# Sliding-window attention and a mixture of experts on one core: the sums of weights move on GpSimd, the half tile's code moves ahead of the full tile's, one tile's turn of x moves

## The chip, the core and the metric

The kernel runs on one NeuronCore of a Trainium2 chip. The metric is the device time of one execution in microseconds (us). Before the change three executions took 769.08, 773.89 and 774.53 us, median 773.89.

The engines of the core run their own instruction streams and meet at semaphores: PE (TensorE, matrix products; its weight loads are shown as PEld), DVE (VectorE), ACT (ScalarE), POOL (GpSimd, which here also issues the gathers and scatters) and SP (SyncE, which issues plain DMAs).

## What is computed

```python
# attention: q, k, v of (8, 8, 576, 64), causal window of 64
scores = where(0 <= i - j < 64, q @ k.T / sqrt(D), -1e9)
attn   = softmax(scores) @ v               # -> x of (4608, 512)
# mixture of experts, one expert per token, E = 8, F = 1024
logits = x @ w_gate;  expert_idx = argmax(logits, axis=1)
gate_w = softmax(logits)[n, expert_idx]
for e in range(E):                         # rows of the tokens of expert e
    h = maximum(x_sorted[lo:hi] @ w1[e], 0)
    y_sorted[lo:hi] = h @ w2[e]
return gate_w[:, None] * y                 # in the tokens' order
```

With the inputs of this case the experts get 669, 400, 748, 505, 592, 390, 566 and 738 tokens.

## The kernel before

**Two parts.** The first (up to about 215 us of the profiled span, with a mixed stretch to 247 us) is the attention. It writes x, already weighted with the gate, to `x_dram`. The second handles tokens expert by expert in *tiles* of 256 slots. Each product of a tile is made with seven smaller products instead of eight (a Strassen scheme), which needs sums and differences of the quarters of the weights and of x.

**A full tile** has these steps, in `body` (L481):

- `finish` (L422): three DVE additions (helper line L380) that complete the output `ys` of the tile *before*.
- `scatter` (L287): POOL copies the token numbers (L288) and issues two indirect DMAs (L291) that write `ys` to `out`.
- `hidden` (L332): PE makes seven products (L340), each 16 matmul records of 128x128. DVE and ACT evict between them (L350, L357, L361, L366, L371 on DVE). Into this stretch DVE also takes twelve of the 16 *transposes* (L311, `turned_blocks`) of the next tile's x, in the slots given by `some(blocks, n)`.
- `output` (L389): DVE forms four sums of the hidden values (`left_sums`, L139), makes the remaining transposes, and PE makes seven products (L384). ACT copies the turned x (L323), DVE forms the sums of the next tile's x (`sums_x`, L329).
- `gather` (L268): after the first product of `output`, POOL copies token numbers (L269) and issues two indirect DMAs (L271), which fetch the x of the tile after the next into the buffer that the transposes have just read.

**A half tile** (`half_tile`, L433) holds up to 160 tokens and is made with plain products: L441 (64 matmul records), L459, L469, L459, with its evictions at L449 and L451, 16 transposes, a gather after them, and L323 and L329 at its end.

**Which tiles run.** Each expert has `tiles` and `fulls`, read into registers at run time. Here they are (3,2), (2,1), (3,3), (2,2), (3,2), (2,1), (3,2), (3,3). Numbering experts from 0 and tiles from t0, the order is: expert 0 two full tiles, which are written out without a test ("first" and "second tile"), then a half one; expert 1 full, half; expert 2 three full; expert 3 two full; expert 4 two full, half; expert 5 full, half; expert 6 two full, half; expert 7 three full. The first tile of experts 1 to 7 is unconditional, all later ones stand inside nested tests made by `more` (L1069).

**Sums of weights.** On POOL, `sums_w1(e)` and `sums_w2(e)` are four operations of 128x1024 each (POOL rows of L139). `hidden` reads the first, `output` the second, whose last sum `t[3]` is used by the second of its products. `sums_w2(e)` stands ahead of the first `body` of expert e, so behind the last gather of expert e-1. `sums_w1(e+1)` stands behind the first tile of expert e. Weights are loaded by SP (L156, L159) at the head of an expert, into buffers of which there are two.

**Order.** Everything is in a schedule written by hand: each engine runs its instructions in the order of the program.

## Time and profile before

| | |
|---|---|
| executions | 769.08, 773.89, 774.53 us |
| the profiled execution | 780.25 us, of it span 778.5 us |
| mean granted TensorE clock over the span | 0.971 |
| a full tile in its undisturbed form, PE start to PE start | 381.53 to 406.12 us: 24.6 us |
| a half tile | 673.40 to 691.39 us: 18.0 us |
| last PE matmul ends, last scatter issued | 766.3 us, 775.2 us |

The profile is of one execution. A row of a group gives busy time and mean ns of one, then the idle time of the engine just ahead of the group and what ended most of it. A row of the timeline gives the start in us from the span's start, the length in us, the engine, the line, the operation with its output and input tiles, how many were merged, and in brackets the idle time ahead of it with what ended it; "issue" means that the profile shows nothing that the engine waited for.

### The profile page before, as it was taken

Reading aid. Unit: us, or ns where it says so; the run is one execution under the profiler, and the core shown is the slowest. Engines: PE = TensorE matmul, PEld = TensorE weight load, DVE = VectorE, ACT = ScalarE, POOL = GpSimd, SP = SyncE. Lnnn points to the kernel's source line nnn. Section 1 sums busy time; section 2 is a strip of 40 time slices with the busy share of each in tenths; the row PEclk is TensorE's granted clock in tenths of the full one; section 3 lists DMA queues with packets and bytes.
Section 4 is the critical chain, followed back from the end, with each engine's and each line's share of the span. In section 5 each row is a group of like instructions: output and inputs, shape, how many; then the busy total and the mean of one; then the engine's idle time right before and its main releaser. Section 6 shows DMA issues by size and latency. Waiting matters only on the chain. (4 is left out here: it accounts for less than half of the span.)

```text
span 778.5 us, 18249 instructions
## 1 busy us (share of the span) xinstructions
PE 707.8 (91%) x6962; PEld 635.1 (82%) x6962; DVE 528.6 (68%) x1654; ACT 267.0 (34%) x676; POOL 356.9 (46%) x366
## 2 busy tenths in 40 slices
PE   5999999999799789998999699899888989999993
PEld 3888888887698678888999599799777879889993
DVE  2677998989667636859667267368496686676862
ACT  4888888887451111102122012022011111112210
POOL 5215476694842426276631534644266527263112
PEclk9999999999999889999999899899999999999997
DMA  8998889883533515144120710711341611111011
GB/s 161 223 203 180 176 204 241 189 237 111 165 108 131 183 59 208 56 149 166 28 69 22 265 28 29 267 35 48 138 154 32 224 62 55 57 30 51 24 42 56
DMA packets 137638, 94.71 MB, mean 122 GB/s; under 512 B 117072, under 2 KB 117072, under 8 KB 137490
## 3 DMA queue, kind: packets, MB, share of 16 engines
q1 hardware_dynamic: 127858, 62.16, 29.4%
q0 software_dynamic: 9056, 28.58, 11.2%
q10 hardware_dynamic: 576, 2.10, 0.8%
q8 instruction: 80, 1.31, 0.8%
q14 instruction: 68, 0.56, 0.2%
HBM read 73.94 MB, written 20.45 MB: 121 GB/s over the span
## 5 line engine op out<-in xcount | busy, mean ns | idle before, releaser
L271 POOL DMA_INDIRECT qk_m<-x_dram,at_g x42 | 45.0, 1070 | 235.6 <-DVE v_m L311 227.4
L311 DVE STREAM_TRANSPOSE v_m<-qk_m 32x256 f32<-32x256 f32 x320 | 139.3, 435 | 12.7 <-DMA qk_m<-x_dram,at_g 7.7
L340 PE MATMUL bank<-qk_m,s 128*128 128x128 f32 x1024 | 129.7, 285 | 19.9 <-DVE qk_m L350 11.7
L340 PEld LDWEIGHTS bank<-qk_m,s 128*128 128x128 f32 x1024 | 124.8, 201 | 21.2 <-issue 14.5
L340 PE MATMUL bank<-qk_m,w 128*128 128x128 f32 x768 | 97.9, 283 | 9.7 <-issue 6.0
L340 PEld LDWEIGHTS bank<-qk_m,w 128*128 128x128 f32 x768 | 94.5, 199 | 11.4 <-issue 10.9
L650 ACT ACTIVATE pr<-pr,mx 128x128 f32<-128x128 f32 x288 | 89.7, 390 | 33.6 <-DVE mx L640 33.3
L640 DVE CUSTOM_DVE_ANT_0 pr<-bank,mask 128x128 f32<-128x128 f32 x288 | 64.4, 285 | 28.5 <-PE bank L627 27.2
L380 DVE TENSOR_TENSOR v_m<-bank,v_m 128x256 f32<-128x256 f32 x95 | 38.2, 420 | 47.2 <-PE bank L384 30.7
L291 POOL DMA_INDIRECT out_dram<-v_m,at_s x42 | 42.4, 1009 | 33.9 <-DVE v_m L380 20.7
L441 PE MATMUL bank<-qk_m,w 128*128 128x160 f32 x320 | 47.9, 312 | 9.7 <-issue 9.7
L139 POOL TENSOR_TENSOR s<-w 128x1024 f32<-128x1024 f32 x22 | 52.7, 2397 | 7.9 <-DMA qk_m<-x_dram,at_g 5.0
L441 PEld LDWEIGHTS bank<-qk_m,w 128*128 128x128 f32 x320 | 46.4, 199 | 12.0 <-issue 12.0
L329 DVE TENSOR_TENSOR qk_m<-v_m,qk_m 128x256 f32<-128x256 f32 x60 | 45.1, 778 | 13.6 <-ACT qk_m L323 13.0
L568 POOL COPY v_m<-v_m 64x520 f32<-64x520 f32 x32 | 19.8, 618 | 67.8 <-DMA v_m<-in_v_dram 65.2
L673 PEld LDWEIGHTS bank<-v_m,pT 128*64 128x64 f32 x1152 | 40.7, 139 | 12.1 <-DVE xs L687 6.0
L673 PE MATMUL bank<-v_m,pT 128*64 128x65 f32 x1152 | 47.4, 230 | 3.1 <-DVE xs L687 3.1
L384 PE MATMUL bank<-qkT_m,v_m 128*128 128x256 f32 x216 | 48.3, 379 | 0.0
L627 PE MATMUL bank<-qkT_m 64*64 64x128 f32 x1152 | 45.8, 290 | 0.1
L384 PEld LDWEIGHTS bank<-qkT_m,v_m 128*128 128x128 f32 x216 | 41.0, 190 | 5.5
L347 ACT COPY qk_m<-bank 128x512 f32<-128x512 f32 x16 | 9.4, 586 | 104.2 <-PE bank L340 86.1
L594 PE MATMUL bank<-ident,qk_m 128*128 128x128 f32 x256 | 36.7, 287 | 7.7 <-POOL mask L516 4.9
(174 smaller groups left out, 1289.0 us busy)
## 6 DMA issues: line engine op xcount, KB each, us to landing
w<-in_moe_w_dram SPq DMA_DIRECT2D x11, 2048.0 KB, 8.5
qk_m<-in_q_dram SPq DMA_DIRECT2D x72, 128.0 KB, 3.6
qk_m<-in_k_dram SPq DMA_DIRECT2D x72, 128.0 KB, 3.6
v_m<-in_v_dram SPq DMA_DIRECT2D x64, 128.0 KB, 3.7
qk_m<-in_moe_w_dram SPq DMA_DIRECT2D x3, 2048.0 KB, 14.3
x_dram<-xs POOLq DMA_DIRECT2D x6, 512.0 KB, 4.9
x_dram<-xs POOLq DMA_DIRECT2D x3, 768.0 KB, 6.1
w<-in_moe_w_dram ACTq DMA_DIRECT2D x4, 512.0 KB, 4.9
```

Source lines behind the costliest of these rows:

```text
L139: op()
L271: G.indirect_dma_start(out=xg[c], out_offset=None, in_=x_dram[:, :], in_offset=bass.IndirectOffsetOnAxis(ap=at_g[:, c : c + 1], axis=0),)
L291: put = G.indirect_dma_start(out=out[:, :], out_offset=bass.IndirectOffsetOnAxis(ap=at_s[:, c : c + 1], axis=0), in_=ys[c], in_offset=None ...
L311: V.transpose(out=xn[b * QD : (b + 1) * QD, :, :, a * QD : (a + 1) * QD].rearrange("p c g i -> p (c g) i"), in_=rows[a * QD : (a + 1) * QD ...
L329: V.tensor_tensor(out=xs[:, n], in0=a, in1=b, op=ALU.subtract)
L340: nc.tensor.matmul(acc[:, f, :], lhsT=a[:, g, f * P : (f + 1) * P], rhs=b[:, g, :], start=(first and f == 0 and g == 0), stop=(g == HG - 1 ...
L384: nc.tensor.matmul(acc, lhsT=a[:, f, :], rhs=b[:, f, :], start=(start and f == 0), stop=(stop and f == HF - 1), skip_group_check=True,)
L441: nc.tensor.matmul(acc[:, i], lhsT=w1[:, g, f * P : (f + 1) * P], rhs=xq[:, g].rearrange("p c s -> p (c s)")[:, 0:HALF], start=(i + g == 0 ...
L627: nc.tensor.matmul(out_, lhsT=qT[rows, t, a * WINDOW : (a + 1) * WINDOW], rhs=rhs, start=True, stop=True, skip_group_check=True,)
L640: V.tensor_tensor_reduce(out=prs[h][:, m, :], in0=scs[h][:, m, :], in1=mask[:, m0 + m, :], scale=-scale, scalar=-2 * MASKED, op0=ALU.add, ...
L650: nc.scalar.activation(out=y, in_=y, func=AF.Exp, scale=-1.0, bias=mx[:, h, m : m + 1])
L673: nc.tensor.matmul(px[a * D : (a + 1) * D, h, m, :], lhsT=pTs[h][:, m, a * D : (a + 1) * D], rhs=vt[:, h, :], start=True, stop=True, skip_ ...
```

## The change

Three edits:

1. `body` takes a function `between`, called after the scatter and ahead of the transposes and the gather. `sums_w2(e)` is handed to the first tile of expert e, `sums_w1(e + 1)` to the next one of the expert (for expert 0, to its half tile), whichever form it has; where there is no such tile a new Else arm calls it. So each set of four POOL operations leaves its old place and stands between L291 and L269 of one tile. Their number doesn't change.
2. The inner test gets `preferred_fallthrough_block=False`. In the built program the half tile's block then stands directly behind the test and the full tile's block behind it, with everything nested in it. Before, the full block with all nested tiles stood first, and each level's half block after all of that.
3. In the second tile of expert 0, `hidden` no longer gets `blocks`: all 16 transposes of that tile are made in `output`, after its `left_sums`.

```diff
-    def body(e, last, after, full):
+    def body(e, last, after, full, between=None):
 
         finish()
         scatter(perm_i[:, last])
+        if between is not None:
+            between()
         blocks = turned_blocks()
...
-        tile1 = chain(hidden(0, blocks), output(0, blocks))
+        tile1 = chain(hidden(0), output(0, blocks))
...
-            if e:
-                sums_w2(e)
-
...
-            def more(n):
-
-                with tc.If(tiles > n):
-                    with tc.If(fulls > n) as full:
-                        body(e, *place(n), True)
+            def more(n, between=None):
+
+                with tc.If(tiles > n) as some_left:
+                    with tc.If(fulls > n, preferred_fallthrough_block=False) as full:
+                        body(e, *place(n), True, between)
                         if n + 1 < KT:
                             more(n + 1)
                         else:
...
                     with full.Else():
-                        body(e, *place(n), False)
+                        body(e, *place(n), False, between)
+                if between is not None:
+                    with some_left.Else():
+                        between()
 
             if e:
-                body(e, *place(0), True)
-            if e + 1 < E:
-                sums_w1(e + 1)
-            more(1 if e else NE)
+                body(e, *place(0), True, partial(sums_w2, e))
+            more(1 if e else NE, partial(sums_w1, e + 1) if e + 1 < E else None)
```

## The prediction

> **What bounds the kernel now.** I read the page first, then the timeline of PE alone over the expert part, then all engines around each gap, then instruction fetches in small windows.

> ```profile
> PE 707.8 (91%) x6962; PEld 635.1 (82%) x6962; DVE 528.6 (68%) x1654; ACT 267.0 (34%) x676; POOL 356.9 (46%) x366
> L340 PE MATMUL bank<-qk_m,s 128*128 128x128 f32 x1024 | 129.7, 285 | 19.9 <-DVE qk_m L350 11.7
> L329 DVE TENSOR_TENSOR qk_m<-v_m,qk_m 128x256 f32<-128x256 f32 x60 | 45.1, 778 | 13.6 <-ACT qk_m L323 13.0
> ```

> PE bounds the expert part: an undisturbed full tile takes 24.6 us from PE start to PE start, with PE never idle. So what can be won is PE's gaps. Summed over the tiles from 246 us on they are about 60 us against 24.6 (full) and 18.0 (half), and come in three kinds.

> First kind, ends of half tiles. L329 has a mean of 778 ns, yet takes 0.42 us in undisturbed tiles:

> ```profile
> 616.14 6.71 DVE L329 TENSOR_TENSOR qk_m<-v_m,qk_m 128x256 f32<-128x256 f32 x3 [0.23 <-ACT qk_m L323]
> 617.66 2.41 POOL L139 TENSOR_TENSOR qkT_m<-qk_m,qkT_m 128x1024 f32<-128x1024 f32 x1
> 622.77 2.56 DVE L329 TENSOR_TENSOR qk_m<-qk_m,v_m 128x256 f32<-128x256 f32 x1
> 627.38 5.15 PE L340 MATMUL bank<-qk_m,s 128*128 128x128 f32 x32 [3.07 <-DVE qk_m L350]
> ```

> The four L329 (both inputs in SBUF) take turns with POOL's four L139, which start after the last gather; finish and L350 queue behind them on DVE, and PE waits for L350.

> Second kind, the second tile:

> ```profile
> 257.33 2.68 DVE L311 STREAM_TRANSPOSE v_m<-qk_m 32x256 f32<-32x256 f32 x6 [6.22 <-DMA qk_m<-x_dram,at_g]
> 262.43 3.79 PE L340 MATMUL bank<-qk_m,s 128*128 128x128 f32 x16 [4.97 <-DVE qk_m L361]
> ```

> DVE stands at the transposes until the gather has landed, and L357 and L361 behind them free PE's banks late.

> Third kind, borders between blocks:

> ```profile
> 283.34 6.90 PE L441 MATMUL bank<-qk_m,w 128*128 128x160 f32 x29 [3.08 <-issue]
> ...
> 436.19 3.38 PE L340 MATMUL bank<-qk_m,w 128*128 128x128 f32 x16 [5.31 <-issue]
> 441.93 2.27 PE L340 MATMUL bank<-qk_m,s 128*128 128x128 f32 x12 [1.91 <-issue]
> 494.38 3.75 PE L340 MATMUL bank<-qk_m,w 128*128 128x128 f32 x16 [3.71 <-DVE v_m L380]
> 770.00 1.27 DVE L380 TENSOR_TENSOR v_m<-bank,v_m 128x256 f32<-128x256 f32 x3 [6.29 <-DMA out_dram<-v_m,at_s]
> ```

> These follow jumps. In windows of about a microsecond the queue "q8 instruction" moves one 16 KB packet at such a place, so I read them as code loading: one at 428.0 to 429.5, two more at 431.0 to 432.5, then PE starts at 436.19. Reading the packets' times against PE's next start, a load from a jump costs 2.7 (half tile at 335.0), 3.3 (548.2), 3.0 (597.5) and 2.9 us (673.4); PE's sequencer is some 2 us ahead of its array, so 0.99, 1.45, 1.16 and 0.62 us show, mean 1.05.

> [...]

> ```profile
> 335.00:344.00 9.00, 9.00 (x66) 8.97 (x67) 6.52 (x17) 0.57 (x1) 7.87 (x7) 1.00 0.11 42
> 436.00:440.00 4.00, 3.81 (x20) 3.78 (x21) 0.00 (x0) 0.35 (x1) 4.00 (x3) 0.62 1.03 400
> ```

> The third number from the end is the granted clock: 1.00 against 0.62.

> **Edit 1, the sums.** Nothing is added; 14 sets of four L139 (4 x 2.35 = 9.4 us) move. Room in a full tile:

> ```profile
> 407.56 1.00 POOL L291 DMA_INDIRECT out_dram<-v_m,at_s  x1 [0.70 <-issue]
> 408.54 0.22 POOL L269 COPY at_g<-perm_i 128x2 int32 x1
> 425.44 1.24 POOL L271 DMA_INDIRECT qk_m<-x_dram,at_g  x1 [16.68 <-DVE v_m L311]
> ```

> The tile's PE start is 406.12: sums could run from +2.5 to +12 us, and the gather behind them on POOL waits for DVE until +19.3 anyway. In a half tile the gather is free at +13.2, so about 1 us is left; later than that, it has some 4 us until the next tile's first transposes. Moved past scatters, the sums also release them: in the tiles after sums_w1 (472.55) the scatter came 5 us late, which nobody waited for; gain zero. In +2.5 to +12 all DVE work is L311 (one input) or evictions with a PSUM input. While POOL ran its old sums at 463 to 472 us those kept their 0.44 and 0.69 us, so I cost the overlap at zero.

> Gain: PE's waits for L350 are 11.7 us (five, the page's row); 1.4 more at 620.50 for L329; the slow matmuls after two of them (5.28 and 5.15 for 3.74) 2.9. Together **16.0**.
> [...] Trace: 2.57 for 0.42 us beside sums of 2.35 to 2.54, so each waits a whole one. [...]
> The new wait: t[3], the *last* of sums_w2, is used at +14.2 (420.36). Before, it was long done. Where a tile follows a half one, finish will come late after a jump (below): end of L329 at about -0.5, 3.2 us of loading, 1.3 of finish, scatter until +5, sums until +14.7. Cost 0.5 us in each of five first tiles, **-2.5**; bounds 0 and -10 (2 us each).

> **Edit 3.** From 246.49 to 279.43 the second tile took 32.9 us, 8.3 too many. Without transposes DVE follows PE through hidden; left_sums end at about +16.8, 16 transposes (0.45 each, 7.2) at +24.0, ACT's copies (1.1) at +25.2, 0.6 to 0.8 after PE could go on. The half tile's transposes wait for a gather issued after them (landing at about 277, median 4.1 us after issue), so its L449 is late by some 0.7. Gain **6.8**; bounds 3 (the gather later still) and 8.

> **Edit 2, the blocks.** A half tile is 160 matmul records and 160 weight loads, a full one 168 and 168. [...]

> Won at entries of half tiles: 0.45 + 3.08 and slow matmuls (11.9 for 8.93) at 280, and 0.99, 1.45 + 0.53, 1.16 + 1.44, 0.62: 6.4 + 6.2 = 12.6. Lost at their exits: four at 0.9 (I take the entry's 1.05 less a longer lead), less the 0.71 that expert 4's exit cost already. [...] Net 12.6 - 3.6 + 0.7 - 4.5 = **5.2**.

> [...]

> Ends of experts without a half tile. Before, two jumps in a row: to the arm of the failed test, and on over the half blocks behind it. After, the second has nothing to pass. Expert 2 to 3: 5.31 + 1.91 + 3.1 of slow matmuls; I leave 0.8 + 1.9 (a block's end is 44 instructions on, and the weights' load is running) + 1.3: gain 6.3. Expert 3 to 4: 3.71 + 3.0 slow, leave 0.8: gain 5.9. Tail: DVE's finish at 770.00 after 6.29 us, about two loads; with one it starts at 766.9: gain 3.1. **15.3**, bounds 5 and 18. [...] For a block end met badly I take **-1**.

> Sum: 16.0 - 2.5 + 6.8 + 5.2 - 3.2 + 15.3 - 1 = 36.6, say 37. The profiled execution, 780.25 us, becomes 743; it lies 0.8% above the median shown, so 773.89 - 37 = **737 us**.

> **Rivals.**
> - *The jumps only move the stalls* (0.14). Entries against exits and double against single jumps cancel, and all seven full jumps show: 16.0 + 6.8 - 7.4 - 2.5 = 13, **761 us**. For it: equal loads, each about 3 us. Against: two-jump chains are in the trace and become one.
> - *Loading is hidden better* (0.08): exits and full jumps free, no late sums: 37 + 8 + 3 + 2.5, **724 us**. For it: expert 4's and 6's old exits showed 0.71 and 0.
> - *The sums come too late in first tiles* (0.05): seven tiles have PE waiting for t[3]. If each L139 took twice its time beside DVE, a set would end at +21.4, 7.2 us late, seven times 50: **787 us**, slower than before. The gain is gone from 5.3 us per tile, when an L139 takes over 4.2 us. Against: 2.34 to 2.54 us beside transposes.
> - *The order of blocks isn't what it says* (0.01): the built program has the half block first.

> **How the numbers follow.** Forecast 0.72 (its own range 726 to 749). The range 724 to 757 leaves out most of the first and third rival. One per cent, about 8 us, is what this measurement can tell from none. Forecast, hidden loading and nearly all of the first rival are faster: 0.93; within 1%: 0.03; slower: 0.04.

> **What would show it.** Right: L329 at 0.42 us throughout and no PE wait for L350 at half tiles; PE's gaps of 5.31 and 3.71 down to about 1; the second tile near 25 us; DVE's last finish within 1 us of PE's end; a double stall at the start of expert 7. Wrong: PE waiting for POOL's L139 by more than 1 us a tile, or gaps over 2 us at jumps into full tiles.

## The result, and the profile after

The changed kernel takes 744.11 us (median of 4 runs, 741.95 to 745.06) against 774.21 us for the kernel before in the same comparison: ratio 0.9615, 95% interval 0.956 to 0.9669. On another chip it gave 741.56 against 773.32 us, ratio 0.9577 (0.9532 to 0.9622). So it saves 30 to 32 us; the prediction said 37 and 737 us. All medians here are of executions in the faster of the chip's two states; of `turn_only` below, two of ten were in the slower one and are left out.

The two profiled executions differ by more, 778.5 to 740.2 us of span, because that of before lay some 6 us above its median and that of after 2 us below. Every place read below comes from single executions, which differ from one another by a few us, and the comparison of totals from the medians.

The page of the changed kernel, first the engines, then two groups (busy us, mean ns | idle us ahead of the group and what ended most of it):

```profile
PE 695.1 (94%) x6962; PEld 625.4 (84%) x6962; DVE 496.7 (67%) x1654; ACT 267.3 (36%) x676; POOL 355.7 (48%) x366
L340 PE MATMUL bank<-qk_m,s 128*128 128x128 f32 x1024 | 124.7, 278 | 0.6 <-issue 0.6
L340 PE MATMUL bank<-qk_m,w 128*128 128x128 f32 x768 | 96.0, 279 | 11.8 <-issue 8.1
```

and the last of these groups as it was before:

```profile
L340 PE MATMUL bank<-qk_m,w 128*128 128x128 f32 x768 | 97.9, 283 | 9.7 <-issue 6.0
```

VectorE's busy time fell by 31.9 us with the same 1654 instructions, and 19.9 us of idle time ahead of the products with `s` fell to 0.6. That ahead of the products with `w`, the first of which opens a full tile, rose from 9.7 to 11.8: stops at jumps moved there. VectorE wasn't the bound; what counted is which of its instructions were late. L329 alone, its shortest, median and longest duration in ns:

```profile
L329 DVE TENSOR_TENSOR qk_m<-v_m,qk_m x60: 415/424/427, 270.6 to 723.5; 128x256 f32<-128x256 f32 x60
```

None of the 60 is over 0.43 us, where the mean before was 0.78.

What is left of TensorE's waits from the second tile on, in the timeline of PE (start, length, idle time ahead of it in brackets with what ended it):

```profile
272.56 2.73 PE L384 MATMUL bank<-qk_m,v_m 128*128 128x256 f32 x8 [3.40 <-DVE v_m L380]
...
295.39 2.02 PE L340 MATMUL bank<-qk_m,w 128*128 128x128 f32 x16 [1.47 <-DMA qk_m<-x_dram,at_g]
...
339.05 2.02 PE L340 MATMUL bank<-qk_m,w 128*128 128x128 f32 x16 [1.15 <-issue]
...
414.51 2.02 PE L340 MATMUL bank<-qk_m,w 128*128 128x128 f32 x16 [1.22 <-DVEq L1070]
...
417.55 1.50 PE L340 MATMUL bank<-qk_m,s 128*128 128x128 f32 x12 [0.57 <-issue]
...
465.54 2.02 PE L340 MATMUL bank<-qk_m,w 128*128 128x128 f32 x16 [0.88 <-DVEq L1070]
...
480.53 1.99 PE L384 MATMUL bank<-qkT_m,qk_m 128*128 128x256 f32 x8 [0.52 <-POOL qkT_m L139]
...
535.73 3.05 PE L340 MATMUL bank<-qk_m,w 128*128 128x128 f32 x16 [1.92 <-issue]
538.57 2.59 PE L340 MATMUL bank<-qk_m,s 128*128 128x128 f32 x16
...
580.75 2.02 PE L340 MATMUL bank<-qk_m,w 128*128 128x128 f32 x16 [0.88 <-issue]
...
648.38 1.02 PE L340 MATMUL bank<-qk_m,w 128*128 128x128 f32 x7 [0.53 <-issue]
651.64 1.49 PE L340 MATMUL bank<-qk_m,w 128*128 128x128 f32 x9 [2.24 <-issue]
652.92 3.40 PE L340 MATMUL bank<-qk_m,s 128*128 128x128 f32 x16
...
703.30 2.05 PE L340 MATMUL bank<-qk_m,w 128*128 128x128 f32 x16 [1.36 <-issue]
```

The reader is to see three things. The wait of 3.40 us in the second tile is new. The 5.31 and 3.71 us at the borders from expert 2 to 3 and 3 to 4 became 1.22 and 0.88. And a full tile behind a half one now pays at its start, as at 535.73, or twice, as at 648.38 and 651.64 after seven matmul records. (The gather named at 295.39 is not what this tile waits for: in `bank3_order` below it starts at 293.85 after 0.75 us, while VectorE gets that gather's rows only at 301.80.)

The end of the run didn't move. VectorE still waits ahead of its last finish:

```profile
731.78 1.27 DVE L380 TENSOR_TENSOR v_m<-bank,v_m 128x256 f32<-128x256 f32 x3 [6.15 <-DMA out_dram<-v_m,at_s]
```

### The profile page after: what moved, and what is told of

Read it like the earlier page. It is cut to its first block, busy times and chain, and to the rows that moved or that the text cites. A ratio compares the mean times of both kernels' runs of the same rounds, so it can differ in the third digit from the quotient of the medians.

```text
span 740.2 us, 18250 instructions
## 1 busy us (share of the span) xinstructions
PE 695.1 (94%) x6962; PEld 625.4 (84%) x6962; DVE 496.7 (67%) x1654; ACT 267.3 (36%) x676; POOL 355.7 (48%) x366
## 3 DMA queue, kind: packets, MB, share of 16 engines
q0 software_dynamic: 9056, 28.58, 11.8%
## 5 line engine op out<-in xcount | busy, mean ns | idle before, releaser
L311 DVE STREAM_TRANSPOSE v_m<-qk_m 32x256 f32<-32x256 f32 x320 | 139.3, 435 | 5.2 <-DMA qk_m<-x_dram,at_g 0.3
L340 PE MATMUL bank<-qk_m,s 128*128 128x128 f32 x1024 | 124.7, 278 | 0.6 <-issue 0.6
L271 POOL DMA_INDIRECT qk_m<-x_dram,at_g x42 | 45.0, 1072 | 165.0 <-DVE v_m L311 155.9
L340 PEld LDWEIGHTS bank<-qk_m,s 128*128 128x128 f32 x1024 | 120.6, 195 | 0.6 <-issue 0.6
L340 PE MATMUL bank<-qk_m,w 128*128 128x128 f32 x768 | 96.0, 279 | 11.8 <-issue 8.1
L340 PEld LDWEIGHTS bank<-qk_m,w 128*128 128x128 f32 x768 | 91.0, 194 | 15.9 <-issue 15.7
L380 DVE TENSOR_TENSOR v_m<-bank,v_m 128x256 f32<-128x256 f32 x95 | 38.2, 420 | 55.3 <-PE bank L384 24.9
L291 POOL DMA_INDIRECT out_dram<-v_m,at_s x42 | 42.5, 1013 | 61.5 <-DVE v_m L380 47.2
L139 POOL TENSOR_TENSOR s<-w 128x1024 f32<-128x1024 f32 x22 | 52.2, 2373 | 0.0
L384 PE MATMUL bank<-qkT_m,v_m 128*128 128x256 f32 x216 | 48.3, 379 | 0.0
L384 PEld LDWEIGHTS bank<-qkT_m,v_m 128*128 128x128 f32 x216 | 41.0, 190 | 5.5
L441 PEld LDWEIGHTS bank<-qk_m,w 128*128 128x128 f32 x320 | 45.1, 194 | 0.4
L441 PE MATMUL bank<-qk_m,w 128*128 128x160 f32 x320 | 45.3, 303 | 0.0
L660 PE MATMUL bank<-ident,pr 128*128 128x128 f32 x288 | 43.8, 290 | 0.0
```

The costliest lines, as they stand in the source:

```text
L139: op()
L271: G.indirect_dma_start(out=xg[c], out_offset=None, in_=x_dram[:, :], in_offset=bass.IndirectOffsetOnAxis(ap=at_g[:, c : c + 1], axis=0),)
L291: put = G.indirect_dma_start(out=out[:, :], out_offset=bass.IndirectOffsetOnAxis(ap=at_s[:, c : c + 1], axis=0), in_=ys[c], in_offset=None ...
L311: V.transpose(out=xn[b * QD : (b + 1) * QD, :, :, a * QD : (a + 1) * QD].rearrange("p c g i -> p (c g) i"), in_=rows[a * QD : (a + 1) * QD ...
L340: nc.tensor.matmul(acc[:, f, :], lhsT=a[:, g, f * P : (f + 1) * P], rhs=b[:, g, :], start=(first and f == 0 and g == 0), stop=(g == HG - 1 ...
L384: nc.tensor.matmul(acc, lhsT=a[:, f, :], rhs=b[:, f, :], start=(start and f == 0), stop=(stop and f == HF - 1), skip_group_check=True,)
```

## The experiments

Length of a tile below means from one TensorE start to the next in the profiled execution. Each ratio is to the kernel before on the same chip.

**One edit at a time.** `sums_only` has edit 1 alone (`between` and its two calls), `layout_only` edit 2 alone (`preferred_fallthrough_block=False`), `turn_only` edit 3 alone (`hidden(0)` for `hidden(0, blocks)`).

> Edit 1 alone: sums between scatter and gather, blocks in the old order, the second tile's transposes in hidden. Theory (POOL's sums and DVE's L329 exclude each other): L329 back to 0.42 us everywhere, no PE wait for L350 at the five half ends, 16 us less of waits and slow matmuls, at most 2.5 back for late sums: 13 to 16 us below before. Rival (the sums were cover, the stall behind half tiles comes back as late code): gain under 5 us. Code loading as before: gaps of about 5.3 and 3.7 us at the two borders stay, and the half tiles' entries.

> Edit 2 alone: the half block ahead of the full one, sums and transposes where they were. Theory (each jump out of the loaded code costs 2.5 to 3.3 us less the sequencer's lead, two in a row cost double): half entries (12.6 us) free, exits 5 to 11 us instead, border of experts 2 and 3 from 10 us to 2, of 3 and 4 from 7 to 1, tail unchanged: 12 to 17 us below before. But exits meet the old waits of L329 there, so part of their cost can hide under it: up to 20. Rival (jumps only move the stalls): within 4 us of before.

> Edit 3 alone: all 16 transposes of the second tile behind left_sums in output. Theory: 32.9 us of the second tile become about 29 as in the changed kernel, where the seventh product of output waits 3.4 us for DVE; the half tile behind it keeps its load of 3.1 us: 3 to 6 us below before. Rival (my estimate before, the tile ends at about 25.4): 7 us below before.

| kernel | median us | ratio | 95% interval |
|---|---|---|---|
| `sums_only` | 759.42 | 0.9822 | 0.976 to 0.9884 |
| `layout_only` | 757.7 | 0.9792 | 0.9754 to 0.9829 |
| `turn_only` | 775.7 | 1.0042 | 1.0008 to 1.0076 |

Against 772.2 us these are -12.8, -14.5 and +3.5 us. The first two are what the theories said or 0.2 us short of it: in `sums_only` no L329 takes over 0.43 us, no product waits for L350, and the borders keep 5.12 and 4.31 us. The third missed both: deferring the transposes alone gains nothing and costs at most 0.8%. The timeline of `turn_only`, second tile:

```profile
263.38 2.47 DVE L139 TENSOR_TENSOR v_m<-qk_m 128x512 f32<-128x512 f32 x1 [0.70 <-ACT qk_m L372]
...
265.25 2.80 POOL L139 TENSOR_TENSOR s<-w 128x1024 f32<-128x1024 f32 x1
265.88 2.72 DVE L139 TENSOR_TENSOR v_m<-v_m,qk_m 128x512 f32<-128x512 f32 x1
...
268.02 2.80 POOL L139 TENSOR_TENSOR s<-w,s 128x1024 f32<-128x1024 f32 x1
268.53 2.83 DVE L139 TENSOR_TENSOR v_m<-qk_m 128x512 f32<-128x512 f32 x1
...
281.69 3.78 PE L384 MATMUL bank<-qk_m,v_m 128*128 128x256 f32 x8 [6.56 <-DVE v_m L380]
```

With the old place of the sums, those of expert 1's first weights run on GpSimd just when VectorE, no longer held up by its transposes, reaches its own additions of the left operand. Here each instruction takes a whole one of the other engine: 2.5 to 2.8 us for 0.69. All 16 transposes follow, and TensorE waits 6.56 us. So edit 3 depends on edit 1, and the three don't add up: -24 us as a sum, -30 together. Edits 1 and 2 without 3 were not run, so what edit 3 adds to them is known from the second tile's length alone.

**Is it the shared access to SBUF, or the length of GpSimd's queue?** Two kernels add work to the changed one at the old place of the second weights' sums (behind an expert's tests).

```diff
+                for _ in range(8):
+                    G.memset(spare[:], 0.0)        # old_place_fill
+                    G.tensor_tensor(out=spare[:], in0=w[:, 0, 0:HD], in1=w[:, 1, 0:HD], op=ALU.subtract)  # old_place_sums
```

(each kernel has one of the two lines in its loop)

> The changed kernel with eight fills of 128 x 512 added on GpSimd at the place which the sums had before; nothing of the result depends on them. Both theories of the sums: GpSimd is busy there but reads nothing from SBUF. If the old sums cost because they keep VectorE from SBUF, VectorE's additions of the left operand (L139) and bank reads (L329) stay at 0.42 us throughout and the total stays within 3 us of 744. If they cost because they stood ahead of the next gather and scatter in GpSimd's queue, the total rises with the fills as it would with sums of the same length.

> The changed kernel with eight subtractions of 128 x 512 from two SBUF operands added on GpSimd at the place which the sums had before, into a tile nobody reads. Theory of the shared read of SBUF: VectorE's L329 and L139 beside them take 1 to 2.7 us for 0.42, TensorE waits again for bank reads (L350 or L329), and the total rises by 8 to 16 us to 752 to 760. Rival (the sums' length in GpSimd's queue counts): total like that of the fills of about the same length.

Single executions: 763.08 and 816.85 us, where the kernel before took 782.48. Both numbers for the totals were wrong, and the added work does not separate the two theories. What TensorE waited for, in us, times and longest, with the fills:

```profile
PE bank L384 <- POOL qkT_m L139: 7.5, 3, 4.7
PE bank L384 <- POOL s L139: 6.3, 3, 4.0
```

and with the subtractions:

```profile
PE bank L384 <- POOL qkT_m L139: 28.5, 3, 11.4
PE bank L384 <- POOL s L139: 26.8, 4, 10.4
```

Both kinds of added work delay the *real* sums, which now stand behind the scatter in the same queue, and TensorE waits for t[3]. Fills of 0.525 us x 8 = 4.2 us in each of seven sets cost 13.8 us of such waits; subtractions of 1.275 x 8 = 10.2 us cost 55.3. Per set that is 4.2 - 2.0 and 10.2 - 7.9: in both cases about 2.2 to 2.3 us of room in GpSimd's queue, on average, and every us beyond it is TensorE's. It is the mechanism of the third rival, with its price: in the changed kernel it shows once, with 0.52 us, but with 10 us more in the queue the kernel is slower than before. About the shared access they only say that single L329 took up to 1.5 us beside subtractions and never over 0.43 beside fills.

So a second form, on the kernel *before*, puts fills in the place of the sums themselves, and so leaves these sums out:

```diff
     def sums_w2(e):
-        form(right_sums(G, s2s[e % NW], *w2q(e)))
+        t = s2s[e % NW]
+        if e:
+            for n in (0, 1, 2, 3, 0, 1, 2, 3, 3):
+                G.memset(t[:, n], 0.0)
+        else:
+            form(right_sums(G, t, *w2q(e)))
```

> The kernel before, with the sums of the second weights of experts 1 to 7 left out: in their place GpSimd makes nine fills of 128 x 1024 of the same tile, which read nothing and take about as long (9 x 1.05 us for 4 x 2.35 us). Theory of the shared access to SBUF: L329 takes 0.42 us throughout, TensorE's waits for L350 at the ends of half tiles (11.7 us) are gone, and the total falls by 10 to 15 us, as when the sums were moved alone. Rival (the length of the sums in GpSimd's queue ahead of the scatter and the next gather): the waits stay, and the total is within 3 us of the kernel before.

755.63 us, ratio 0.9759 (0.9717 to 0.98): 17.7 us less than before, 2.7 above the upper end of what was expected. The rows of the groups:

```profile
L334 DVE TENSOR_TENSOR qk_m<-v_m,qk_m 128x256 f32<-128x256 f32 x60 | 23.7, 422 | 13.7 <-ACT qk_m L328 13.0
L156 POOL MEMSET s<- 128x1024 f32 x36 | 32.7, 963 | 7.3 <-DMA qk_m<-x_dram,at_g 5.0 <-issue 2.1
```

(L334 and L156 are L329 and the fills there.) Nine fills of 0.96 us, 8.7 us per set, hold the queue nearly as long as four sums of 2.35, at the same place, and the 60 additions are back at 422 ns; TensorE waits for L350 at no half tile's end. Reading from SBUF on both engines at once was the cost, not the place in the queue: VectorE's additions took 2.5 to 2.8 us beside sums of 2.8 in `turn_only`, and 0.42 beside fills here. Why the total fell by 5 us more than in `sums_only` isn't separated: a set is 0.7 us shorter, and TensorE multiplies zeros there.

**The new wait in the second tile.** Products yy and yx2 are the two halves of one PSUM bank, yps[2], that is bank 7. `after_bank3` puts yx2 into bank 3:

```diff
-    yy, yx2 = (yps[2][:, h] for h in (lo_, hi_))
+    yy = yps[2][:, lo_]
+    yx2 = banks[3](0, DM)[:, hi_]
```

> The changed kernel with yx2, the output of the seventh product, in another PSUM bank (3, which the first tile alone used) and not in the bank of yy, which DVE reads late in the second tile. Theory (PE waits there for DVE's read of yy in the same bank): the wait of 3.40 us ahead of L384 at 272.6 and the slow matmuls behind it go, PE of the half tile then waits for ACT's copies only: 2.5 to 4 us below the changed kernel, 32 to 42 below before. Rival (PE waits for DVE's value, not for the bank): unchanged.

738.21 us, ratio 0.9558 (0.9504 to 0.9613), 34.0 us below before as expected; the ratio's interval overlaps that of the changed kernel, so the gain over it isn't shown by the totals. The wait of 3.40 us is gone, and the second tile is 25.21 us long, where it was 29.04. The changed kernel's timeline of VectorE shows why it waited:

```profile
262.76 7.17 DVE L311 STREAM_TRANSPOSE v_m<-qk_m 32x256 f32<-32x256 f32 x16
270.62 1.22 DVE L329 TENSOR_TENSOR qk_m<-v_m,qk_m 128x256 f32<-128x256 f32 x3 [0.68 <-ACT qk_m L323]
271.75 0.42 DVE L329 TENSOR_TENSOR qk_m<-qk_m,v_m 128x256 f32<-128x256 f32 x1
272.09 0.94 DVE L380 TENSOR_TENSOR v_m<-bank,v_m 128x256 f32<-128x256 f32 x2
```

The first of the two L380 reads yy, behind 16 transposes and four L329. TensorE's seventh product starts only when that read is through, at 272.56, though it writes the other half of the bank: the wait of 3.40 us. In `after_bank3`, with that product in another bank, it starts at 271.49, 3.1 us ahead of the read at 274.59.

Most of the gain is lost again two tiles later. In `after_bank3`, expert 1's first tile has

```profile
307.41 2.02 PE L340 MATMUL bank<-qk_m,s 128*128 128x128 f32 x16 [2.85 <-DVE qk_m L361]
```

and is 27.76 us long, where the changed kernel has 24.67. From the second tile's start to that tile's end it is 72.8 us against 74.0. So the cause of the wait is shown, but removing it alone moved most of it; more on this under `bank3_order`.

**The tail.** `no_last_gather` leaves out the gather of expert 7's third tile (`fetch=not (e == E - 1 and n == 2)`).

> Leaves out one gather: that of the following tile's rows, issued within expert 7's third tile, whose rows no tile uses with these counts. Prediction's theory of the tail (VectorE waits for the code of a taken jump): the tail from the last tile's first transpose group to the end is unchanged at 12.0 us, with VectorE's first finishing step still idle for about 6 us; total 744 us. Theory formed on the trace of the changed kernel (the failed test waits until the last gather has landed, at 729.3 us, and only then raises the scatter's semaphore, which VectorE waits for): that idle time falls by 2 to 5 us, the tail to 8 to 10 us, total 740 to 742 us.

749.13 us, ratio 0.9591 (0.9539 to 0.9642), on a chip where the kernel before took 782.48. The reason was right, the gain not there: the tail behind TensorE's last matmul is 13.6 us long, 12.1 in the changed kernel. In the changed kernel the chain of waits that ends last (start, us, what) reads:

```profile
724.28 5.03 DMA qk_m<-x_dram,at_g
729.31 0.02 issue
729.33 0.04 POOLq L1070
729.37 2.19 another core or an unknown queue
731.56 0.10 POOLq L1070
```

and GpSimd's own instructions in the test's line (shortest/median/longest ns):

```profile
L1070 POOLq EVENT_SEMAPHORE  x15: 17/43/5676, 408.3 to 729.3; - x15
L1070 POOLq INC_SWDGE_SEM  x3: 1210/1376/2238, 414.3 to 729.4; - x3
```

The arm that isn't taken waits for the last gather to land (729.31) and then spends 2.2 us in an INC_SWDGE_SEM, which the chain lists as an unknown queue; VectorE's finish starts right behind it. Without that gather, in `no_last_gather`:

```profile
735.22 1.27 DVE L380 TENSOR_TENSOR v_m<-bank,v_m 128x256 f32<-128x256 f32 x3 [3.23 <-DVEq L1071]
```

The idle time falls from 6.15 to 3.23 us. TensorE's last matmul ends at 734.5 there, so the finish now stands 0.7 us behind it, against 3.6 us in the changed kernel. But the run doesn't end earlier, since GpSimd's last drain (longest of three, ns) took over, first of the changed kernel:

```profile
L1114 POOLq DRAIN  x3: 40/117/3403, 735.8 to 740.0; - x3
```

then of `no_last_gather`:

```profile
L1115 POOLq DRAIN  x3: 40/117/10545, 736.8 to 747.9; - x3
```

What this drain waits for, 10.5 us where the other traces have 3.0 to 3.4, the profile doesn't show. It is no transfer of this core: from 741 us on its DMA engines are idle. It stays open. Nor is it shown whether VectorE also waited for code in the 6 us, unseen behind GpSimd.

**Does the double stop depend on where the code lies?** `moved_code` adds five small matmuls at the end of the second tile, 20 TensorE instructions, so that all later code lies 20 further on.

```diff
         for _ in tile1:
             pass
+        for _ in range(5):
+            nc.tensor.matmul(banks[3](0, 8), lhsT=ident[:], rhs=ident[:, 0:8], start=True, stop=True, skip_group_check=True)
```

> The changed kernel with five matmuls of 8 columns added at the end of the second tile, so that all later TensorE instructions lie 20 further on in the program; nothing reads them, and they take under 1 us. Theory of the fetched blocks: the stop in expert 7's first tile behind a half tile (0.53 and 2.24 us and matmuls at 3.4 us, the tile 28.8 us long) moves away, and that tile is 25 to 26 us long, while the second stop at the border from expert 2 to 3 (0.57 us) changes by up to 1 us; total 741 to 743 us. Rival (the stop is the taken jump's own and does not depend on where the code lies): that tile stays at 28 to 29 us, and the total is 744 to 745 us.

748.2 us, ratio 0.9566 (0.9508 to 0.9623). Its timeline of PE, at the border from expert 2 to 3 and at the starts of experts 6 and 7:

```profile
422.35 1.46 PE L340 MATMUL bank<-qk_m,w 128*128 128x128 f32 x11 [0.72 <-DVEq L1072]
425.42 0.82 PE L340 MATMUL bank<-qk_m,w 128*128 128x128 f32 x5 [1.60 <-issue]
...
589.66 2.63 PE L340 MATMUL bank<-qk_m,w 128*128 128x128 f32 x16 [2.75 <-issue]
...
658.86 2.02 PE L340 MATMUL bank<-qk_m,w 128*128 128x128 f32 x16 [0.23 <-issue]
```

The stop of 2.24 us in expert 7 is gone and that tile is 25.55 us long, not 28.81; at the other border the second stop comes after 11 matmul records where it came after 16 + 4 = 20, and grew from 0.57 to 1.60 us. Nine records, each with its weight load, are 18 instructions, about the 20 by which the code moved. Both are as the theory of the fetched blocks expected, and the rival is out: what these two jumps cost depends on where the code lies. How long a block is wasn't shown. But the stop at the start of expert 6 grew from 0.88 us (1.37 in `after_again`) to 2.75. So part of what one jump gained another lost. The five matmuls took 1.9 us, not under 1, and the total was not the 741 to 743 us expected, on a chip where the kernel before took 782.48; by its ratio it can't be told from the changed kernel's.

**Together.** `bank3_order` is `after_bank3` with the last two of the second weights' sums exchanged, so that t[3] is ready 2.4 us earlier; `bank3_moved` adds the five matmuls to it, in bank 6. `after_again` is the changed kernel on the same chip.

```diff
-        for n, (a, b) in enumerate(((b12, b11), (b22, t[:, 0]), (b22, b12), (t[:, 1], b21))):
+        for n, (a, b) in ((0, (b12, b11)), (1, (b22, t[:, 0])), (3, (t[:, 1], b21)), (2, (b22, b12))):
```

> The changed kernel once more, on the same chip as the three others of this call, so that they can be set against it. Expected: a ratio to the kernel before of 0.955 to 0.97, and the gaps of its first trace: 3.4 us in the second tile, a double stop in expert 7's first tile, VectorE idle for 6 us at the end.

> The changed kernel with the seventh product of the output half in bank 3, and the last two sums of the second weights in reversed order, so that the one which TensorE reads first of the late ones is ready 2.4 us earlier. Theory: the wait for the bank in the second tile (3.4 us) and the single wait for the late sum (0.5 us) are gone; 4 to 6 us below the changed kernel of the same call, ratio to the kernel before 0.950 to 0.960. Rival: the wait for the last sum only changes places with one for the other sum, and the total is that of the kernel with bank 3 alone (0.956) or above.

> As the last, with the five small matmuls that move the code of the later tiles by 20 instructions, into bank 6. Theory of the fetched blocks: the double stop of expert 7's first tile goes (3 us), the small matmuls cost 1 to 2 us, and the border from expert 2 to 3 changes by up to 1 us; 0 to 2 us below the kernel without them. Rival: other tiles lose as much at the moved edges of blocks, and the total is 1 to 3 us above it.

| kernel | median us | ratio | 95% interval |
|---|---|---|---|
| `after_again` | 741.56 | 0.9577 | 0.9532 to 0.9622 |
| `bank3_order` | 738.0 | 0.9519 | 0.9484 to 0.9555 |
| `bank3_moved` | 738.99 | 0.9521 | 0.9483 to 0.9558 |

`after_again` came as expected, with the same 3.40 us and the double stop (0.38 + 2.20 us). `bank3_order` lies 3.6 us below it, less than the 4 to 6 expected, with intervals that overlap. No wait for a late sum is left in its trace. The exchange also adds a few TensorE instructions (seven in the executed program, six of them ahead of expert 7), and the double stop there is gone without any small matmul (0.27 us, the tile 24.67 long). In its place expert 6 starts with 3.24 us, as in `moved_code`. Moving the code again in `bank3_moved` brings nothing: expert 6 starts with 3.27 us, and the total is 1.0 us above, by the medians what its rival said. What `after_bank3` lost in expert 1's first tile is lost here too, where the timeline of `bank3_order` has

```profile
282.55 2.39 POOL L139 TENSOR_TENSOR s<-w 128x1024 f32<-128x1024 f32 x1
...
292.63 1.02 POOL L271 DMA_INDIRECT qk_m<-x_dram,at_g  x1 [0.27 <-POOL at_g L269]
...
301.80 2.68 DVE L311 STREAM_TRANSPOSE v_m<-qk_m 32x256 f32<-32x256 f32 x6 [3.34 <-DMA qk_m<-x_dram,at_g]
...
306.98 1.41 PE L340 MATMUL bank<-qk_m,s 128*128 128x128 f32 x5 [2.18 <-DVE qk_m L361]
...
581.63 2.02 PE L340 MATMUL bank<-qk_m,w 128*128 128x128 f32 x16 [3.24 <-issue]
```

In expert 0's half tile the sums now hold the gather on GpSimd until 292.63. Its second half is issued at 293.96, and VectorE has its rows only at 301.80, 7.8 us later (in the changed kernel that half lands 4.7 us after its issue at 290.76); SP had issued a weights' load of 2 MB at 293.18, between the two halves, where in the changed kernel it comes after both. In the next tile VectorE stands at the transposes for 3.34 us and TensorE waits 2.18 us: that tile is 28.64 us long instead of 24.67. How much is the sums' and how much the load's isn't separated. Sums behind the gather in that one half tile would be the next thing to try; it wasn't tried.

## Why the prediction was right, and where its sum was off

The direction holds, and so do the mechanisms of edit 1, of the borders and of the half tiles' entries. The forecast of 37 us was 5 to 7 us too much. Term by term, in the order of the text, from the two profiled executions:

| term | predicted us | measured us |
|---|---|---|
| sums, waits for L350 and L329 with the slow matmuls | +16.0 | +16.0 (the waits, 13.1, are gone, and matmuls there at 3.74 again) |
| new wait for t[3] | -2.5 | -0.5 |
| edit 3 | +6.8 | +3.0 (32.9 us became 29.0, and the half tile behind has 0.9 of slow matmuls) |
| entries of half tiles | +12.6 | +12.6 (all gone) |
| exits of half tiles, less the one old exit | -7.4 | -11 |
| jumps into full tiles | -3.2 | about -1.7 |
| border 2 to 3 | +6.3 | +8.3 |
| border 3 to 4 | +5.9 | +5.2 |
| tail | +3.1 | +0.1 |
| a block's end met badly | -1 | counted with its place |

These make about 32 of the 38.3 us between the two spans. Five stops of 0.15 to 0.33 us in the half tiles' L469, which are gone, make 1.4 more; the other 5 are spread over tiles in which I can't name a wait. That the terms' sum came within 5 us of the forecast is partly luck: edit 3, the exits, the tail and one border together came out 11 us worse than forecast, and the other terms 6.5 us better.

- *Sums.* The step "the four L329 take turns with POOL's four L139" was right and is shown by `before_fills`. That the overlap at +2.5 to +12 us costs nothing was right too: beside the sums in expert 1's first tile six transposes took 2.67 us (0.45 each), and a sum took 2.36 to 2.41.
- *t[3].* Placed wrong, and smaller. It was expected in the five first tiles behind a half tile. It came once, 0.52 us, behind a border without one, where GpSimd stood in the failed test's arm, the scatter came at 468.68 and the sums ended at 480.5. The added work showed that the room is 2.2 us a set, so the worry had a basis.
- *Edit 3.* The step "0.6 to 0.8 after PE could go on" looked only at the next consumer of the transposes. It missed that yy's read queues behind them on VectorE, and that the seventh product needs yy's bank: 3.40 us, and slower matmuls after it. `after_bank3` shows it. Of the five signs that the prediction named for being right, this tile (29.0 us for 25) and the last finish (3.6 us behind TensorE's end for 1) failed.
- *Exits.* "four at 0.9" was too little: 1.47, 1.15, 1.92 and 0.88 us, mean 1.36, with 1.7 us of slow matmuls behind the longest. The net sum's 4.5 us for a double stop into expert 7 is a term that no run shows a source for; in its place the changed kernel's trace has 0.53 + 2.24 us there and 1.9 us of slow matmuls.
- *Slow matmuls.* They could not be forecast from a gap's length. Before, gaps of 2.39 us (at 313.07) and 3.07 us (627.38) were followed by a granted clock of 0.71 and 0.73 over the product behind them, gaps of 2.48 us (362.22) and 3.06 us (576.87) by 1.00. In the changed kernel the product at 535.73, behind 1.92 us, has 0.63. So the slow matmuls in these terms are those of single executions: in `after_again` the same tile at 537.17 starts after 1.44 us and has none.
- *Full tiles.* The term of -3.2 us was the author's estimate (three of the seven jumps at the entries' 1.05), and no run shows it; in its place one of seven jumps showed over 1 us (1.36 at 703.30), others 0.1 or nothing.
- *Borders.* Two jumps became one, as said; left were 1.22 + 0.57 us, the second behind 20 matmul records as in the trace of before (1.91 us at 441.93), and 0.88 us.
- *Tail.* This step failed in its cause, so its gain of 3.1 us didn't come. "About two loads" took VectorE's idle 6.29 us for code loading. The row itself names a DMA of the scatter; it is GpSimd's arm of the failed test, held by the last gather. The layout of code did not change that: the tail of `layout_only` is 12.5 us long, that of before 12.2.

Of the rivals, "the jumps only move the stalls" has part of the truth: what entries gave, exits nearly took back (12.6 against 11). But the whole of edit 2 still gave 14.5 us by itself, because of the borders: in `layout_only` the four tiles around the two are 15.2 us shorter than before. Code loading itself is inferred from the packets and from the moved code: in `moved_code` one double stop went (2.24 us in expert 7) and the other came nine records earlier, while expert 6's stop grew from 0.88 to 2.75 us.

## What to carry to other kernels

When two engines both read SBUF with two operands, look at the *shortest* instructions of the one that isn't the bound: a mean of nearly twice the minimum (0.78 for 0.42 us here) can mark the collision, and moving the other engine's work to a stretch with PSUM operands or transposes removed it here (0.43 us at most) without removing any work. Before work is deferred on an engine, follow every instruction queued behind it, not only its own consumer: a late read of half a PSUM bank held the next product into the other half for 3.40 us here. A stop at a jump can move to another jump when instructions are added (20 took 2.24 us away in expert 7 and made 0.88 into 2.75 in expert 6), so weigh all jumps, not the one that was cured. And an idle engine behind a test that fails need not be waiting for code (6.15 us became 3.23 here without the last gather): read the chain of the engine that reaches it last, and what that arm itself waits for.
